# Twenty tail-value products moved into the first segment, tail rows loaded earlier, second scores placed inside a value chunk

## The chip, the cores and the metric

The kernel runs on one core of one Trainium2 chip. The metric is the device time of one execution in microseconds (us). A core has five engines that run beside each other and wait for each other through semaphores: TensorE (PE in the profile; its weight loads are listed apart as PEld), VectorE (DVE), ScalarE (ACT), GpSimd (POOL) and SyncE (SP), whose queue issues most of the transfers (DMAs).

## The reference, cut to what matters

The input x has 2048 rows of 640. The first block is a memory-augmented transformer with 32 heads of 128. The rows are cut into 64 segments of 32; ahead of each segment stand 8 memory rows, so that each attention covers 40 rows:

```
for s in range(64):
    h = concat([mem, layernorm(x)[32*s : 32*s + 32]])      # 8 + 32 rows
    q, k, v = h @ Wq, h @ Wk, h @ Wv                       # 640 -> 32 heads x 128
    p = softmax(mask(q @ k.T * scale));  o = (p @ v) @ Wo
    mem = o[:8];  outs.append(o[8:])
h  = x + concat(outs)
h2 = h + (relu(layernorm(h) @ w1 + b1)**2) @ w2 + b2       # w1: 640 -> 1728
```

Segment s + 1 needs the memory rows that segment s has produced: the 64 segments are a chain. The feed-forward part at the end is not.

## The kernel before, in words

**Sixteen blocks of four segments.** `step(b, sp)` works on segment s = 4b + sp. It projects 32 rows at a time: the 8 memory rows and the first 24 rows of the segment (`HD`). The last 8 rows of each segment, the tail rows (`TL`), depend on no memory; the tail rows of a whole block, four times 8, are projected together, as *tail units*: one unit is one 128-row chunk c of the contraction with four products of 128x32 by 128x512, which run beside each other in the four 32-column groups of PE. Ten units make the q, k or v of a block's tail rows (two halves n of five chunks). Finished v halves go through a row tile to a DRAM buffer `vt_d` (`tail_out`, L363) and come back per block as `vt`. Ten more units per block apply Wo to the tail rows of a block that is done.

**One step.** q and k of both halves (`project`, L498), with `first_half` (L609) inside the last of them: `scores(0)` and `soft1(0)`. Scores `sm` are those of the 8 memory queries only (16 small products, L526); the others, `token_scores`, are weighed a step later, off the chain. Then the value projection of half 0 into `ps0`, with `token_scores(0)` in its middle, `soft2(0)`, `scores(1)`, `soft1(1)`, `soft3`, whose four copies of 32 rows spread the transposed weights into `pB` (L566: g = 0 on DVE, g = 1 on ACT, g = 2 and 3 on POOL), then the value projection of half 1 into `ps1` in two pieces around `token_scores(1)` (L648 to L652). `values(0)` (weights times v, 20 products on PE), `values_out(0)` (a cast to `oT` on ACT), `values(1)`, and the output rounds `wo_rounds` into `pw`, whose first 16 products read the oT of half 0. `wo_out` (L298) turns pw into the next memory rows: two copies on ACT, a sum on DVE and a transpose into `hT` (L412), which the q projection of the next step reads. The weighted values of the 32 rows of the step before (`token_values`, on PE) come between.

**The filler.** Tail units and tail-output units are put into the list `fill`, which `step` empties at fixed places with `run(fill, n)`: (ahead - 1)//2 of them ahead of `values(0)` (L680), the rest of `ahead` between `values(0)` and the output rounds (L685), and what is left after the output rounds (L727). `ahead` is half of the list, rounded up (L678). How many a step gets is set by `portion(s)` (L951): the total up to step s is round(8.05 s), so mostly 8, from `plan`, sorted by due time, with an earliest step for each entry (L942 to L947).

**An instruction count per step.** `lack` (L590) keeps the number of PE products per step at 1911/5 = 382.2 on average, by splitting up to 12 sets of projection products per projection into halves of 256 columns. A split set streams the same columns in twice as many instructions.

**The front.** `start` (L845) projects v, q and k of the first 32 rows together with the tail rows of blocks 0 to 3, and fills with tail-v units of blocks 4 to 9; the first step then has `ready` set, projects nothing and runs only its chain, with 5 units left over (`run(fill, 10)`, L665; `SEG0` at L796 holds zeros). SP issues in program order: rows 0 to 127 of x, three chunks of Wv, tail rows of x for blocks 4 to 7 (group 1), a chunk of Wv, group 2, the last chunk, Wq, Wk, Wo, then the writes to vt_d. ACT's queue issues tail rows of group 0 and the memory rows `mem0` (L139, L140). DVE works in order: statistics of the first rows (`ln_stats(0)`, L905), spreading mem0 into o0 (L907), the normalisation `ln_norm(0)` (L193), the transpose of the memory rows (L412), and only then statistics and normalisation of tail group 0 (L914). PE transposes the rows (L210), ACT and DVE copy them out. Group 3 (tail rows of blocks 12 to 15) is loaded in the first blocks, by four small DMAs, and transposed by a DMA.

Of the kernel before, what the change touches and what calls it, by code (L numbers as in the profile page):

```python
# [16 lines left out]
def kernel(  # L17
# [107 lines left out]
    def load_tail_rows(g, eng=nc.sync):  # L125

        xt = s2.tile([128, D], BF16, tag="xt", name="xt")
        if g > 2:
            for b in range(4):
                eng.dma_start(out=xt[32 * b:32 * b + 32, :],  # L130
                              in_=x2d.rearrange("(b s t) d -> b t s d", s=4, t=SEG)[4 * g + b, HD:SEG, :, :])
        else:
            eng.dma_start(out=xt[:], in_=x2d.rearrange("(s t) d -> s t d", t=SEG)[16 * g:16 * g + 16, HD:SEG, :])
        xts["t", g] = xt
# [4 lines left out]
    load_tail_rows(0, nc.scalar)  # L139
    nc.scalar.dma_start(out=mem0[HD:SEG, :], in_=A_mem0[0])  # L140
    load_w(wv, A_Wv, 0, 3)
# [55 lines left out]
    def ln_transpose(b):  # L197

        xn = xns.pop(b)
        if not isinstance(b, tuple) and b > 0:  # L200
            nc.sync.dma_start(out=rows_in(b), in_=xn[:], transpose=True)
            return
        if isinstance(b, tuple) and b[1] > 2:
            hTt = s2.tile([128, DC, 4, TL, 4], BF16, tag="hTt", name="hTt", bufs=4)
            nc.sync.dma_start(out=hTt[:].rearrange("p c b k s -> p c (b k s)"), in_=xn[:], transpose=True)
# [23 lines left out]

    def proj(w, by, lhs, n, ps, c0, c1):  # L230

# [6 lines left out]
        for c in range(c0, c1):  # L238
            for k in range(4):
                out_, rhs, start, stop = ps[32 * k:32 * k + 32, :], wr[:, c, n, k], c == 0, c == DC - 1  # L240
                if owed[0] == 0 or start or stop:
                    matmul(out_, lhsT=lhs(c), rhs=rhs, start=start, stop=stop)
# [243 lines left out]
    def step(b, sp, v=None):  # L486
# [39 lines left out]
        def scores(n):  # L526
            sm = chn.tile([128, 512], F32, tag="ch", name="sm")
            for j, g in [(j, g) for a in range(2) for j in range(4) for g in (a, a + 2)]:
                p = n * 16 + g * 4 + j
                matmul(sm[32 * g:32 * g + 32, 0:NK], lhsT=qz[:, p, :], rhs=of(kT, p),  # L530
                       start=(j == 0), stop=(j == 3), skip_group_check=True)
            sms[n] = sm
# [28 lines left out]
        def soft3(pm):  # L561
            pT = s1.tile([128, 2, 32], BF16, tag="pTt", name="pT")[:].rearrange("p u k -> p (u k)")
            nc.vector.transpose(out=pT, in_=pm)
            def part(g):
                r = slice(32 * g, 32 * g + 32)
                (nc.vector.tensor_copy, nc.scalar.copy, nc.gpsimd.tensor_copy, nc.gpsimd.tensor_copy)[g](out=pBs[0][r, g], in_=pT[r])  # L566
            for g in range(1, G):
# [40 lines left out]

        def first_half():  # L609
            if not last:  # L610
                scores(0)
# [17 lines left out]
        def token_scores(n):  # L629
            skv = view()  # L630
            for j in range(4):
                for g in range(G):
                    matmul(skv[32 * g:32 * g + 32, n * 4 + j, :], lhsT=of(qT, n * 16 + g * 4 + j),
                                     rhs=of(kT, n * 16 + g * 4 + j), start=True, stop=True,
                                     skip_group_check=True)

        token_scores(0)
# [12 lines left out]
        token_scores(1)  # L650
# [13 lines left out]
        if ready:  # L664
            run(fill, 10)  # L665
            run_late(0, 100)
# [178 lines left out]
    def start():  # L845
# [43 lines left out]

        owed[0] = 72  # L890
        stream("q", wq, qT, lambda: ln_transpose(("t", 2))())
# [51 lines left out]
    for b in range(10, NB):  # L943
        u = tail_units(b, "v")
        plan += [(b - 8 if b < 12 else 28 + 4 * (2 * b - 24 + n), 1 if b < 12 else 7, u[DC * n:DC * n + DC]) for n in range(2)]
    for b in range(NB - 1):
# [4 lines left out]
    def portion(s):  # L951
        n = {NS - 3: 482, NS - 2: 486}.get(s, round(8.05 * s)) - paced[0]
        got = []
        while True:
# [6 lines left out]
            d, _, u = begun[0]  # L961
            if len(got) >= min(n, 9) and d > s:
                break
# [6 lines left out]
    for b in range(NB):  # L970
        for sp in range(4):
# [17 lines left out]
            if 0 < b < NB - 1 and sp == 1:  # L989
                ln_transpose(b + 1)  # L990
            if (b, sp) == (0, 3):
                load_tail_rows(3)
            if (b, sp) == (1, 0):
                late.insert(0, (1.15, lambda: ln_stats(("t", 3)), 4))
            if (b, sp) == (1, 1):
                mid.append(lambda: ln_norm(("t", 3)))
            if (b, sp) == (1, 2):
                ln_transpose(("t", 3))
            e = b * 4 + sp - (NS - 7)
# [144 lines left out]
```

## Time and profile before

| | us |
|---|---|
| median of three runs | 938.44 (937.07 to 940.75) |
| the profiled execution | 941.83 |
| its span in the trace | 940.0 |
| PE busy | 917.0 (98%) |
| PEld busy | 593.6 (63%) |
| DVE busy | 627.6 (67%) |
| ACT busy | 607.9 (65%) |
| POOL busy | 308.5 (33%) |

The profiled execution took 1.8 us more than its span. Busy time says which engine works, not whether it works at its rate: PE counts as busy while a product is under way, and products of neighbouring column groups overlap. The timeline lists start and duration of merged groups of instructions; an entry in brackets is the idle time of the engine before the group and what ended it. "SPq" rows are issues of transfers, not transfers.

### The profile page before, as it was taken

How to read it: one execution, taken by the hardware profiler on the slowest of the kernel's cores; microseconds unless marked ns; L12 is line 12 of the kernel's file. 1: busy time of each engine (PE TensorE's matmuls, PEld its weight loads, DVE VectorE, ACT ScalarE, POOL GpSimd, SP SyncE). 2: the span in 40 equal slices, each digit the busy share in tenths (PEclk: the TensorE clock that was granted, in tenths of full speed). 3: DMA queues.
4: the chain of work that ended last, by engine and by line, in shares of the span. 5: the costliest groups of instructions: out<-in, count | busy, mean ns of one | idle time of the engine just before them, and what ended most of it. 6: DMA issues, size and time to landing. Idle time of an engine off the chain costs nothing.

```text
span 940.0 us, 58306 instructions
## 1 busy us (share of the span) xinstructions
PE 917.0 (98%) x25889; PEld 593.6 (63%) x25900; DVE 627.6 (67%) x2068; ACT 607.9 (65%) x1586; POOL 308.5 (33%) x1003
## 2 busy tenths in 40 slices
PE   5989999999999999999999999999999999999998
PEld 2546666666666666666666666666666666565555
DVE  4257777767777677777777777767677777556632
ACT  1557777777777777777777777777777766524321
POOL 2123333333333333333333333333333343344300
PEclk9999999999999999999999999999999999999999
DMA  9982212020201010110102010101010221724320
GB/s 348 411 277 68 45 15 32 12 29 16 27 16 25 20 22 20 20 22 23 23 15 32 10 32 13 32 14 33 14 33 13 52 44 23 259 58 92 92 57 29
DMA packets 65820, 56.80 MB, mean 60 GB/s; under 512 B 37320, under 2 KB 61648, under 8 KB 63648
## 3 DMA queue, kind: packets, MB, share of 16 engines
q1 hardware_dynamic: 65280, 52.57, 21.1%
q8 instruction: 203, 3.33, 1.5%
q14 instruction: 49, 0.40, 0.2%
q10 hardware_dynamic: 160, 0.17, 0.1%
q0 software_dynamic: 128, 0.33, 0.1%
HBM read 38.37 MB, written 9.44 MB: 51 GB/s over the span
## 4 chain that ended last, share of the span: by engine, by line
PE 96%; DVE 2%; ACT 1%; DMA 1%; issue 1%; POOL 0%; ACTq 0%; DVEq 0%
PE ps L228 31%; PE px L228 22%; PE pw L228 16%; PE pk L228 7%; PE ps L1045 6%; PE po L228 5%; PE y L1101 4%; PE ps L1101 2%; PE sm L228 2%; PE pa L228 1%; DMA mem<-in_A_mem_dram 1%; DVE wk L1054 0%; ACT row L268 0%; DVE lnst L158 0%; PE pe L228 0%
## 5 line engine op out<-in xcount | busy, mean ns | idle before, releaser
L228 PEld LDWEIGHTS <-hT 128*32 128x32 bf16 x8764 | 218.8, 96 | 121.1 <-DVE hT L412 20.3
L228 PE MATMUL px<-wv,hT 128*32 128x512 bf16 x2520 | 173.4, 378 | 0.0
L228 PE MATMUL pw<-wo,oT 128*32 128x320 bf16 x4224 | 169.6, 299 | 0.3 <-ACT oT L259 0.2
L228 PEld LDWEIGHTS <-oT 128*32 128x32 bf16 x4224 | 112.5, 96 | 36.9 <-ACT oT L259 20.7
L711 POOL TENSOR_TENSOR pkt<-ek,rk 128x64 bf16<-128x64 bf16 x64 | 18.9, 295 | 254.6 <-ACT otmp L311 253.0
L282 DVE STREAM_TRANSPOSE qT<-row 128x256 f32<-128x256 f32 x128 | 56.8, 443 | 64.8 <-ACT row L266 64.7
L282 DVE STREAM_TRANSPOSE kT<-row 128x128 f32<-128x128 f32 (+1 forms) x191 | 68.0, 357 | 30.0 <-ACT row L268 19.0
L228 PE MATMUL ps<-wq,hT 128*32 128x512 bf16 x1266 | 81.2, 382 | 2.1 <-DVE hT L412 1.7
L228 PEld LDWEIGHTS <-hTt 128*32 128x32 bf16 x1976 | 59.7, 97 | 33.4 <-issue 6.1
L228 PEld LDWEIGHTS <-v 32*128 32x128 bf16 (+1 forms) x4064 | 58.5, 93 | 35.0 <-issue 24.7
L1053 ACT ACTIVATE wv<-ps,b1f 128x512 bf16<-128x512 f32 (+1 forms) x56 | 37.6, 671 | 65.9 <-PE ps L1045 65.1
L228 PE MATMUL ps<-wk,hT 128*32 128x512 bf16 (+1 forms) x1695 | 80.2, 327 | 0.0
L228 PE MATMUL px<-wq,hT 128*32 128x512 bf16 (+1 forms) x1895 | 79.3, 308 | 0.0
L228 PE MATMUL pk<-wk,hT 128*32 128x512 bf16 (+1 forms) x1252 | 77.6, 377 | 0.0
L463 ACT CAST oT<-po 128x512 bf16<-128x512 f32 x128 | 68.7, 589 | 12.1 <-PE po L228 5.8
L266 ACT ACTIVATE row<-ps 128x512 bf16<-128x512 f32 x93 | 69.2, 771 | 4.5 <-PE ps L228 3.3
L259 ACT CAST oT<-po 128x128 bf16<-128x128 f32 x126 | 33.4, 265 | 52.9 <-PE po L228 51.4
L475 POOL COPY qz<-qT 128x96 bf16<-128x96 bf16 x126 | 33.4, 265 | 103.8 <-DVE qT L282 102.7
L519 ACT CAST row<-ps 128x256 bf16<-128x256 f32 x126 | 48.4, 457 | 20.4 <-PE ps L228 20.4
L266 ACT ACTIVATE row<-px 128x512 bf16<-128x512 f32 x63 | 47.5, 754 | 21.3 <-PE px L228 21.3
L310 ACT COPY otmp<-pw 64x96 f32<-64x96 f32 (+2 forms) x129 | 28.8, 223 | 50.0 <-PE pw L228 29.6
L228 PEld LDWEIGHTS <-qz 128*32 128x32 bf16 x2016 | 40.0, 94 | 26.8 <-issue 12.1
(143 smaller groups left out, 1856.6 us busy)
## 6 DMA issues: line engine op xcount, KB each, us to landing
wv<-in_A_Wv_dram SPq DMA_DIRECT2D x5, 1024.0 KB
wq<-in_A_Wq_dram SPq DMA_DIRECT2D x5, 1024.0 KB
wk<-in_A_Wk_dram SPq DMA_DIRECT2D x5, 1024.0 KB
o_all<-o SPq DMA_DIRECT2D x256, 7.5 KB
wo<-in_A_Wo_dram SPq DMA_DIRECT2D x6, 640.0 KB
vt<-vt_d SPq DMA_DIRECT2D x15, 256.0 KB
xt<-in_A_x_dram SPq DMA_DIRECT2D x18, 160.0 KB
wq<-in_B_w_dram SPq DMA_DIRECT2D x1, 2080.0 KB
```

The costliest lines, as they stand in the source:

```text
L228: nc.tensor.matmul(*args, **kw)
L259: nc.scalar.copy(out=out_, in_=in_)
L266: nc.scalar.mul(out=paired(row), in_=ps.rearrange("p (s f) -> p s f", s=2), mul=scale)
L282: nc.vector.transpose(out=to[:, n * 8 + u0 * 4:n * 8 + u1 * 4, 0:32], in_=row.bitcast(F32).rearrange("p (h e) -> p h e", e=32)[:, u0 * 4:u ...
L310: nc.scalar.copy(out=five(tmp[0:64])[:, cs], in_=blocks(64, 128, 0)[:, cs])
L463: nc.scalar.copy(out=oTg[:, gs, :, :, 0:SEG], in_=po[1][h][:, :, 0:256].rearrange("p g (n j q) -> p g n j q", n=2, q=32))
L475: nc.gpsimd.tensor_copy(out=d[:, :, :, 0:120].rearrange("p s g (j f) -> p s g j f", j=3)[:, :, :, :, 0:M], in_=src[:, :, :, 0:3])
L519: nc.scalar.copy(out=paired(row[:])[:, :, fs], in_=ps[:].rearrange("p (s f) -> p s f", s=2)[:, :, fs])
L711: nc.gpsimd.tensor_tensor(out=pkt[:], in0=ek[:, :, SEG:NK], in1=rk[:].unsqueeze(2).to_broadcast([128, HG, TL]), op=ALU.mult)
L1045: nc.tensor.matmul(ps[:], lhsT=w1[:, c, fc * 128:(fc + 1) * 128], rhs=hnT[:, c, :], start=(c == 0), stop=(c == DC - 1))
L1053: nc.scalar.activation(out=r[:, 0:w], in_=ps[:, 0:w], func=ACT.Relu, bias=b1f[:, fc:fc + 1], scale=1.0)
L1101: nc.tensor.matmul(y[hh][:, 0:DH], lhsT=f1T[:, fc, k * 128:(k + 1) * 128], rhs=w2[:, fc, cs], start=(fc == 0 and q == 0), stop=(fc == FFUL ...
```

## The change

- The memory rows are issued by SP, second in its queue and ahead of Wv, rather than by ACT. The statistics of tail group 0 stand ahead of the spreading of mem0 on DVE.
- Tail group 3 is loaded by one DMA behind the first chunk of Wk, its statistics and normalisation stand between the q and the k part of `start`, and PE transposes it in the k part. Its four DMAs, its work and its DMA transpose in blocks 0 and 1 go.
- The tail-v units of blocks 10 and 11 may begin at step 0. `portion` gives step 0 twenty units and then 7.717 per step rather than 8.05. In step 0, 5 units are run at the old place, 16 between the output rounds and 4 after them.
- Of the filler of a later step, 4 units are always left for after the output rounds, the rest goes ahead of them.
- The first chunk of `ps1` is cut by columns into two parts (heads 0 and 3, heads 1 and 2); `scores(1)` stands between the parts. Scores go through all four column groups in turn for each j, rather than through two groups first and then the other two.
- The copy g = 3 of `soft3` goes from POOL to DVE.
- `lack` gets a constant of 43; 76 rather than 72 sets are split in the q part of `start`.

```diff
-        if g > 2:
-            for b in range(4):
-                eng.dma_start(out=xt[32 * b:32 * b + 32, :], in_=...)
-        else:
-            eng.dma_start(out=xt[:], in_=x2d...[16 * g:16 * g + 16, HD:SEG, :])
+        eng.dma_start(out=xt[:], in_=x2d...[16 * g:16 * g + 16, HD:SEG, :])
...
-    nc.scalar.dma_start(out=mem0[HD:SEG, :], in_=A_mem0[0])
+    nc.sync.dma_start(out=mem0[HD:SEG, :], in_=A_mem0[0])
...
-        if isinstance(b, tuple) and b[1] > 2:
-            hTt = s2.tile([128, DC, 4, TL, 4], BF16, tag="hTt", name="hTt", bufs=4)
-            nc.sync.dma_start(out=hTt[:]..., in_=xn[:], transpose=True)
-            hTts[b[1]] = hTt
-            return
...
-    def proj(w, by, lhs, n, ps, c0, c1):
+    def proj(w, by, lhs, n, ps, c0, c1, part=None):
...
+                if part is not None:
+                    js = slice(1, 3) if part else slice(0, 4, 3)
+                    matmul(out_.rearrange("p (j e) -> p j e", j=4)[:, js], lhsT=lhs(c), rhs=rhs[:, js],
+                           start=(start and part == 0), stop=False, skip_group_check=True)
+                    continue
...
-            for j, g in [(j, g) for a in range(2) for j in range(4) for g in (a, a + 2)]:
+            for j in range(4):
+                for g in range(G):
...
-   (nc.vector.tensor_copy, nc.scalar.copy, nc.gpsimd.tensor_copy, nc.gpsimd.tensor_copy)[g](...)
+   (nc.vector.tensor_copy, nc.scalar.copy, nc.gpsimd.tensor_copy, nc.vector.tensor_copy)[g](...)
...
-            lack = paces[0] + (1911 * (len(paces) - 1)) // 5 - issued[0]
+            lack = paces[0] + (1911 * (len(paces) - 1)) // 5 - issued[0] + 43
...
             pm0 = soft2(0)
+        if not ready:
+            ps1 = potile(1)
+            proj(wv, "half", lhs, 1, ps1, 0, 1, 0)
+        if not last:
             scores(1)
...
-            ps1 = potile(1)
-            proj(wv, "half", lhs, 1, ps1, 0, 2)
+            proj(wv, "half", lhs, 1, ps1, 0, 1, 1)
+            proj(wv, "half", lhs, 1, ps1, 1, 2)
...
-            run(fill, 10)
+            run(fill, SEG0[9])
...
-            ahead = 0 if ready else (len(fill) + 1) // 2
+            ahead = 0 if ready else max(len(fill) - 4, 0)
...
-    SEG0 = (0, 0, 0, 0, 0, 0, 0)
+    SEG0 = (0, 0, 6, 2, 2, 3, 3, 0, 0, 5)
...
-        owed[0] = 72
+        owed[0] = 76
...
+        ln_stats(("t", 3))
+        ln_norm(("t", 3))
...
-        stream("k", wk, kT)
+        stream("k", wk, kT, lambda: ln_transpose(("t", 3))())
...
     ln_stats(0)
+    ln_stats(("t", 0))
...
     mem_to_hT(o0, 0, 0)
-    ln_stats(("t", 0))
...
-    load_w(wk, A_Wk)
+    load_w(wk, A_Wk, 0, 1)
+    load_tail_rows(3)
+    load_w(wk, A_Wk, 1, DC)
...
-        plan += [(b - 8 if b < 12 else ..., 1 if b < 12 else 7, ...) for n in range(2)]
+        plan += [(0 if b < 12 else ..., b // 12, ...) for n in range(2)]
...
-        n = {...}.get(s, round(8.05 * s)) - paced[0]
+        n = {...}.get(s, round(20 + 7.717 * s)) - paced[0]
...
-            if len(got) >= min(n, 9) and d > s:
+            if len(got) >= min(n, 9 if s else 20) and d > s:
```

The inner places of `SEG0` stand ahead of the groups of output rounds of step 0, its last place is the old `run(fill, 10)`. The removed lines of the main loop (`load_tail_rows(3)` at block 0, its statistics, normalisation and DMA transpose in block 1) are not repeated here.

More of the change, by code (lines that the diff above doesn't have):

```diff
@@ L127, in load_tail_rows @@
         xt = s2.tile([128, D], BF16, tag="xt", name="xt")
-        if g > 2:
-            for b in range(4):
-                eng.dma_start(out=xt[32 * b:32 * b + 32, :],
-                              in_=x2d.rearrange("(b s t) d -> b t s d", s=4, t=SEG)[4 * g + b, HD:SEG, :, :])
-        else:
-            eng.dma_start(out=xt[:], in_=x2d.rearrange("(s t) d -> s t d", t=SEG)[16 * g:16 * g + 16, HD:SEG, :])
+        eng.dma_start(out=xt[:], in_=x2d.rearrange("(s t) d -> s t d", t=SEG)[16 * g:16 * g + 16, HD:SEG, :])
         xts["t", g] = xt
@@ L202, in ln_transpose @@
             return
-        if isinstance(b, tuple) and b[1] > 2:
-            hTt = s2.tile([128, DC, 4, TL, 4], BF16, tag="hTt", name="hTt", bufs=4)
-            nc.sync.dma_start(out=hTt[:].rearrange("p c b k s -> p c (b k s)"), in_=xn[:], transpose=True)
-            hTts[b[1]] = hTt
-            return
         pt = mm.tile([128, 1024], BF16, tag="mm", name="pt")
@@ L240, in proj @@
                 out_, rhs, start, stop = ps[32 * k:32 * k + 32, :], wr[:, c, n, k], c == 0, c == DC - 1
+                if part is not None:
[3 more added lines that the diff above has]
+                    continue
                 if owed[0] == 0 or start or stop:
-                    matmul(out_, lhsT=lhs(c), rhs=rhs, start=start, stop=stop)
+                    matmul(out_, lhsT=lhs(c), rhs=rhs, start=start, stop=stop, skip_group_check=(by == "half"))
                     continue
@@ L527, in scores @@
             sm = chn.tile([128, 512], F32, tag="ch", name="sm")
-            for j, g in [(j, g) for a in range(2) for j in range(4) for g in (a, a + 2)]:
-                p = n * 16 + g * 4 + j
-                matmul(sm[32 * g:32 * g + 32, 0:NK], lhsT=qz[:, p, :], rhs=of(kT, p),
-                       start=(j == 0), stop=(j == 3), skip_group_check=True)
+            for j in range(4):
+                for g in range(G):
+                    p = n * 16 + g * 4 + j
+                    matmul(sm[32 * g:32 * g + 32, 0:NK], lhsT=qz[:, p, :], rhs=of(kT, p),
+                                     start=(j == 0), stop=(j == 3), skip_group_check=True)
             sms[n] = sm
@@ L565, in part @@
                 r = slice(32 * g, 32 * g + 32)
-                (nc.vector.tensor_copy, nc.scalar.copy, nc.gpsimd.tensor_copy, nc.gpsimd.tensor_copy)[g](out=pBs[0][r, g], in_=pT[r])
+                (nc.vector.tensor_copy, nc.scalar.copy, nc.gpsimd.tensor_copy, nc.vector.tensor_copy)[g](out=pBs[0][r, g], in_=pT[r])
             for g in range(1, G):
@@ L609, in first_half @@
         def first_half():
+            if ready:
+                run(fill, SEG0[7])
             if not last:
@@ L635, in token_scores @@
                                      skip_group_check=True)
+        if ready:
+            run(fill, SEG0[8])
         token_scores(0)
@@ L944 @@
         u = tail_units(b, "v")
-        plan += [(b - 8 if b < 12 else 28 + 4 * (2 * b - 24 + n), 1 if b < 12 else 7, u[DC * n:DC * n + DC]) for n in range(2)]
+        plan += [(0 if b < 12 else 28 + 4 * (2 * b - 24 + n), b // 12, u[DC * n:DC * n + DC]) for n in range(2)]
     for b in range(NB - 1):
@@ L951, in portion @@
     def portion(s):
-        n = {NS - 3: 482, NS - 2: 486}.get(s, round(8.05 * s)) - paced[0]
+        n = {NS - 3: 482, NS - 2: 486}.get(s, round(20 + 7.717 * s)) - paced[0]
         got = []
@@ L990 @@
                 ln_transpose(b + 1)
[L991 to L998, printed above, removed]
             e = b * 4 + sp - (NS - 7)
```

## The prediction, made blind

> **What bounds the kernel now.** I read first the page (busy shares, the forty slices), then the timeline of the first 64 us, then that of one step in the middle, and last the same places of all steps.
>
> ```profile
> PE 917.0 (98%) x25889; PEld 593.6 (63%) x25900; DVE 627.6 (67%) x2068; ACT 607.9 (65%) x1586; POOL 308.5 (33%) x1003
> ...
> PE   5989999999999999999999999999999999999998
> DMA  9982212020201010110102010101010221724320
> ...
> q8 instruction: 203, 3.33, 1.5%
> ```
>
> PE is busy everywhere but in the first slices, where the transfers are too: the weights. So the time is PE's work plus PE's waits, and a moved product gains only where it fills a wait. The front shows two such places:
>
> ```profile
> 8.88 0.45 DVE L193 TENSOR_SCALAR xn<-xt,lnmv,lnrs 128x640 bf16<-128x640 bf16 x1
> ...
> 11.77 0.45 DVE L193 TENSOR_SCALAR xn<-xt,lnmv,lnrs 128x640 bf16<-128x640 bf16 x1 [1.00 <-POOL lnrs L166]
> ...
> 12.92 1.04 PE L228 MATMUL pa<-wv,hT 128*32 128x512 bf16 x8
> ```
>
> PE's first projection waits for the second normalisation (tail group 0), 2.9 us behind the first. Then step 0:
>
> ```profile
> 58.83 0.28 PE L228 MATMUL po<-pB,v 128*32 128x32 bf16 x16 [0.78 <-DVE pB L558]
> 58.93 0.24 PE L228 MATMUL po<-pB,vt 128*32 128x128 bf16 x4
> 59.06 2.56 PE L228 MATMUL pw<-wo,oT 128*32 128x320 bf16 x64
> 62.81 1.30 PE L228 MATMUL ps<-wq,hT 128*32 128x512 bf16 x20 [1.19 <-DVE hT L412]
> ```
>
> The output rounds run without a hole; the 1.19 us behind them wait for the new memory rows. A step in the middle:
>
> ```profile
> 483.04 0.83 PE L228 MATMUL px<-wv,hT 128*32 128x512 bf16 x12
> 483.12 0.62 DVE L282 STREAM_TRANSPOSE kT<-row 128x128 f32<-128x128 f32 x2
> 483.69 0.31 PE L228 MATMUL sm<-kT,qz 128*32 128x40 bf16 x11
> 483.82 0.40 PE L228 MATMUL px<-wv,hT 128*32 128x512 bf16 x2
> 484.66 0.51 POOL L566 COPY pB<-pT 32x64 bf16<-32x64 bf16 x2 [1.04 <-DVE pT L563]
> 485.22 0.27 PE L228 MATMUL po<-pB,v 128*32 128x32 bf16 x11
> 485.67 0.27 ACT L259 CAST oT<-po 128x128 bf16<-128x128 f32 x1
> 486.03 0.79 PE L228 MATMUL pw<-wo,oT 128*32 128x320 bf16 x16
> ```
>
> The second scores start as the two kT transposes end. From values(0) (485.22) to the output rounds are 0.80 us, in which three filler units run; the rounds need the cast, which starts 0.45 us after values(0). From one first k product (pk) to the next, 42 of the first 59 steps take 11.75 to 11.93 us, the others up to 12.15.
>
> **Part 1, the front: -3.2 us at PE's first projection.** mem0 makes DVE wait: it lands on DVE at 7.17, and four copies of 0.94 and four of 0.70 us stand ahead of xn at 8.88. Ahead of Wv on SP it lands behind x's first rows, whose statistics start at 2.98. DVE then has: statistics 2.98 to 4.11; those of group 0, whose last packets land at 4.26, from about 4.6 to 5.7 (0.88 + 0.21); the copies to 7.35; xn at 7.4, 1.5 earlier; 0.66 us of small work (0.18, 0.34, 0.14); xn of group 0 at 8.3 rather than 11.77, its POOL work done long before. That is -3.5. The price is on SP: the mem0 transfer waits for the clearing of mem0 on DVE, which ends at 1.18, and Wv, issued at 1.19, goes behind it, by about 0.45 us, and all weights with it. The last Wv chunk landed at 18.38 and was first used at 22.59; it lands at 18.9 and with some 0.4 us to the semaphore meets a use at 19.1. I take -3.2. By their packets, Wq and Wk had 5.9 to 7.4 us between landing and use; 3.2, 0.45, and 0.5 for group 3 (160 KB at the 0.4 MB/us of these slices) fit in.
>
> The profile's rows give a clock of 1.00 from 12 to 21 us, but sets of four 512-column products start 0.43 us apart until 18.28 and 0.216 after it. If the slow pace ended at 18.28 whenever PE begins, only half of the 3.2 would be kept. [...]
>
> **Part 2, step 0: +3.9 us of which 4.26 come back.** Five more transposes on PE in start cost 0.27 (five take 0.28 of PEld at 26.06); their evacuation, 1.03 us on ACT and 0.74 on DVE, lies in a stretch where ACT is half busy (11.0 of 22 us). The statistics of group 3 (1.6 us of DVE) fall where DVE has 3 of 22 us busy. Sixteen units of 0.213 (four products of 512 columns beside each other) between the output rounds are 3.41 us and fill nothing that is a hole now; the last four lie in the hole of 1.19 and are free. They hold up one thing: the evacuation of the third tail row on ACT (0.58) stands ahead of wo_out's copies, +0.25. Do they cover Wo? Its last packets land at 59.3 now, about 60.7 to 61 with 0.45 + 0.5 ahead of them and the semaphore; PE, 2.9 earlier at 56.1, reaches the last group at 61.9. So they do, with 1 us to spare; without them it would wait to 61. The first k product of step 1, at 63.93 now, comes at 63.93 - 3.2 + 0.27 + 3.41 + 0.25 = 64.7, **+0.75**. Four writes of rows to vt_d on SP are ahead of step 1's vt load and of two loads of x; the row ring of four lets the k row of step 1 wait for the fourth write (issued near 64.3, a few us for such writes); bounds 0 and 2 us, I take 0, as 128 KB writes of this shape at 62.5 were through by 65.5.
>
> **Part 3, the filler: -2.4 rather than -4.26 us.** The listing of PE's order gives 20 units (4.26 us) less after step 0; in 16 steps only two units (0.40 to 0.43 us) are left between values(0) and the rounds. Values(0) itself takes 0.163. With three units this is 0.80: no wait. With 0.533 us of units (values(0) at 414.25, rounds at 415.02) it is 0.765, 0.069 more than their work; with 0.400 (769.98 to 770.68) 0.705. So the cast's floor is 0.705 to 0.765, and two units would need 0.59. Each of these steps wins 0.04 to 0.10, not 0.213. I take 0.765, the row with the same 0.445 from values(0) to the cast as the tail units show. Where the rounds start late, values(1) and the rest take 0.043 less (values(1) to the last product 1.68 for 1.735, 0.01 back ahead of it). Behind the rounds the floor is the chain to hT: last round to first q is 1.486 us for units of 0.267 to 0.853, so four units are just enough; the change keeps 0.77 to 0.93 there. Summed step by step with these floors: -1.8, and -0.6 for values(1). Both ends: -4.3 (no floor) and -1.2 (none of the help of part 5).
>
> **Part 4, second scores: -2.7 us.** From the first product of scores(1) to that of token_scores(1) takes 0.577 (median), from scores(0) to token_scores(0) 0.534 for the same products; 0.043 in each of 60 steps, and in a dozen the scores come another 0.035 or so late: 3.2 in all. It is the second kT transpose: the old order could begin on the first one. With half a chunk ahead (four 256-column products, 0.109) PE comes at 483.79, the transposes have ended at 483.74; the new order needs both from its second product on. The split costs 0.003 a step by rows (six such sets take 0.655, three whole ones 0.648). Bounds: 0 (the wait stays) to -3.2. The strided halves are not in the trace; their columns are the same.
>
> **Part 5, the copy g = 3.** Scores end 0.012 later, and PE reaches values(0) 0.043 earlier, where POOL's second copy now ends 0.05 ahead of it (485.17, 485.22). On DVE the copy adds some 0.09 behind 484.56; ACT's at 485.06 is then last, and values(0) does not wait. Without it 0.05 a step, 2.9 us, would go. It is in part 3's floors (0.345 from the last value product to values(0) becomes 0.285).
>
> **Sum.** +0.75 - 2.4 - 2.7 = -4.4 us. The profiled 941.83 (span 940.0 and 1.8 around it) becomes 937.4; it lies 3.4 above the median, so on the median 938.44 I say **934.0**.
>
> **Rivals.** *The filler is worth its full time:* 4.3 for 2.4, 931.8; against it, the 0.765 row. *The front gives half or nothing* (tail rows of x or Wv late, the slow pace lasting to 18.28): 1.6 to 3.2 lost, 936.5; for it, the last Wv chunk with no slack. *The value chain gives part 4 back:* +2.9, 937; for it, slack of some 0.06. *Slower: pauses of PE's instruction stream.* Queue q8 brings 203 blocks of 16.4 KB for 52,033 instructions, one per 256. In 14 of 62 steps PE, by the start times of its products, pauses 0.14 to 0.47 us (mean 0.27) near row 194 of a block: in ten behind the last round (row 184 to 193 in most steps), in four shortly ahead of it. After the change the last round has row 190 to 230, mostly above 196, so the pause falls within the rounds, ahead of the chain to hT. Should it come in every step there, 48 more times 0.27 make +13, 947; it turns slower from 17 more such pauses. Against: of the 19 old steps with a row above 194, four paused in the rounds, no larger a share than ten of the others. [...] *The change doesn't do what it says:* the listing has the scores between the halves, and 20 units in step 0.
>
> **How the numbers follow.** Forecast 0.48 (own range 932 to 936), full filler 0.15, front 0.20, value chain 0.08, pauses 0.09. About 0.5% (4.7 us) can be told from no change. Half of the forecast and the full filler are beyond it: 0.39; slower 0.09; the rest 0.52. The range 930.5 to 938.5 leaves out the pauses and the tails.
>
> **What would show it.** First projection at 9.5 to 9.9; first pk near 64.7; scores(1) to token_scores(1) 0.534; values(0) to the rounds 0.77 in the two-unit steps; as many pauses as now. Wrong would be: pk of step 1 past 66, or a rounds' end with pauses in most steps.

## The result

| | before | after |
|---|---|---|
| median of ten runs | 938.74 us (937.07 to 940.75) | 943.07 us (940.67 to 949.17) |
| the profiled execution | 941.83, span 940.0 | 943.79, span 941.7 |
| start of the first projection | 12.92 | 9.40 |
| start of the first k product (pk) of step 1 | 63.93 | 66.38 |
| from there to the end of the 61 steps behind it | 724.2 | 723.8 |

The ratio is 1.0050 (95% interval 1.0035 to 1.0065): slower, by 4.3 us, where 934.0 had been forecast. The profiled execution of before lies 3.1 us above its median, that of after 0.7, so the two profiles differ by less than the medians do. The first projection did start earlier, yet step 1 started later, and the chain behind it took as long as before. The next two parts follow the front and the chain.

### The front and step 0

The timeline of the first 22 us after the change (start, duration, engine, line, operation; in brackets the idle time ahead and what ended it):

```profile
7.38 0.33 DVE L407 STREAM_TRANSPOSE hT<-o 128x160 bf16<-128x160 bf16 x1
...
9.40 1.04 PE L218 MATMUL pa<-wv,hT 128*32 128x512 bf16 x8
...
12.56 0.38 PE L218 MATMUL pv<-wv,hTt 128*32 128x512 bf16 x4
...
17.12 0.61 PE L218 MATMUL pa<-wv,hT 128*32 128x512 bf16 x8 [0.73 <-DMA wv<-in_A_Wv_dram]
...
20.10 0.62 PE L218 MATMUL pa<-wv,hT 128*32 128x512 bf16 x8 [1.07 <-DMA wv<-in_A_Wv_dram]
```

PE starts 3.5 us earlier and then waits twice for Wv. By the packets of the trace the last two chunks of Wv were through at 15.36 and 18.33; PE got them at 17.12 and 20.10, 1.76 us later each time. In the trace the end of each of these loads is 16 increments of a semaphore. For the fourth chunk 15 of them had come by 16.04, the last at 17.08; for the last chunk 14 had come by 18.95, the other two at 20.03 and 20.06: PE waited for the last ones. In the thirteen profiles of kernels with the new front, the waits for Wv ended 1.4 to 3.0 us after the last packet. Step 0, from the timeline of PE:

```profile
57.24 1.50 PE L218 MATMUL pw<-wo,oT 128*32 128x320 bf16 x32
58.57 1.47 PE L218 MATMUL ps<-wv,hTt 128*32 128x512 bf16 x24
...
63.64 1.03 PE L218 MATMUL ps<-wv,hTt 128*32 128x512 bf16 x15
65.25 1.30 PE L218 MATMUL ps<-wq,hT 128*32 128x512 bf16 x27 [0.58 <-DVE hT L407]
66.38 1.26 PE L218 MATMUL pk<-wk,hT 128*32 128x512 bf16 x32
```

The rounds begin 1.82 us earlier than before (59.06), not 2.9, and from there to the first q product (the group with the bracket) takes 8.01 us instead of 3.75: 4.26 more. That is as much as twenty units take, though only sixteen stand there; the rest is explained further down.

### The chain

Two steps of after side by side, PE in the timeline. First one that runs without a break in its output rounds (pw), then the step before it, 12 us earlier:

```profile
181.91 0.23 PE L218 MATMUL po<-pB,vt 128*32 128x128 bf16 x4
181.97 1.82 PE L218 MATMUL pw<-wo,oT 128*32 128x320 bf16 x48
183.62 1.12 PE L218 MATMUL ps<-wo,oTt 128*32 128x320 bf16 x28
```

```profile
169.47 0.23 PE L218 MATMUL po<-pB,vt 128*32 128x128 bf16 x4
169.53 1.81 PE L218 MATMUL pw<-wo,oT 128*32 128x320 bf16 x45
171.85 0.32 PE L218 MATMUL pw<-wo,oT 128*32 128x320 bf16 x3 [0.51 <-issue]
171.87 1.17 PE L218 MATMUL ps<-wk,hTt 128*32 128x512 bf16 x16
```

The same in the weight loads (PEld), which go ahead of the products:

```profile
170.08 0.93 PEld L218 LDWEIGHTS <-oT 128*32 128x32 bf16 x30 [0.17 <-ACT oT L254]
171.86 0.10 PEld L218 LDWEIGHTS <-oT 128*32 128x32 bf16 x2 [0.85 <-issue]
```

After 30 of the last weight loads PE stands still for 0.85 us with "issue" as the releaser: it waits for nothing that the profile shows. The profile's page says the same of all steps in one line; first before, then after (busy us, mean ns, then idle time ahead and its releaser):

```profile
L228 PE MATMUL pw<-wo,oT 128*32 128x320 bf16 x4224 | 169.6, 299 | 0.3 <-ACT oT L259 0.2
```

```profile
L218 PE MATMUL pw<-wo,oT 128*32 128x320 bf16 x4224 | 174.2, 300 | 5.5 <-issue 3.8
```

Setting the steps side by side by the start times of their products shows the pauses. The stretch from the first values(1) product to the last round takes 1.682 us where nothing disturbs it (before 1.735), that from the last round to q 1.487; what a step takes beyond that is counted as pause. Of 60 steps, before has 14 pauses, of 3.7 us in sum, ten of them behind the rounds; **after has 24, of 11.1 us, all but 0.1 us of it in the rounds** (counted from the first values(1) product), the longest 1.0 us. The steps without a pause became shorter, as forecast: their median was 11.78 us and is 11.67.

That these are late instruction blocks can be read from the transfers. Queue q8, which the page lists as "instruction", made 204 transfers of 16.4 KB in this profile. PE has 52,301 records in it (26,036 weight loads, as many products, 229 of its sequencer), 256.4 for each transfer, so a block is counted here as 256 instructions of PE; the *row* is an instruction's place in its block. Among the 22 gaps of over 0.33 us between weight loads of one group that wait for no semaphore, all 22 stand at row 194 or 195 of a block, and PE goes on 1.24 to 1.56 us after the end of a q8 transfer. In no run of this case did PE pass that row of a block sooner than 1.1 us after the end of the transfer ahead of it. Three steps of after (those that begin at 150.41, 197.93 and 162.08 us), times in us from their first k product, from the packets of q8 and the weight loads:

```
begin    q8 transfers                          row 194 in the rounds: reached, left
150.41   1.59-2.77   5.84-6.95   9.52-10.59    no pause
197.93   1.79-2.74   6.80-7.79  10.79-11.67    8.78, 9.22
162.08   1.53-2.76   6.92-8.38  10.89-12.00    8.83, 9.78
```

The transfer ahead of the rounds starts at 5.8 in the step without a pause and at 6.8 or later in the other two, and its end decides. In 59 steps of this profile row 194 falls in the rounds: in 36 of them that transfer has ended by 7.37 us, and none pauses by over 0.1 us; in the other 23 it ends at 7.79 or later, and all pause. In the chain the next transfer never starts sooner than 2.18 us after the end of the one before, and all but one in twenty take 0.88 to 1.4 us (the longest 1.9). From start to start a round of this supply takes at least 3.2 us in all runs, with a median of 3.8, and a step of 11.7 us needs three rounds.

### The profile page after: what moved, and what is told of

Same layout as the page of the kernel before. It is cut to its first block, busy times and chain, and to the rows that moved or that the text cites. A ratio compares the mean times of both kernels' runs of the same rounds, so it can differ in the third digit from the quotient of the medians.

```text
span 941.7 us, 58591 instructions
## 1 busy us (share of the span) xinstructions
PE 917.9 (97%) x26036; PEld 559.9 (59%) x26036; DVE 635.9 (68%) x2132; ACT 612.5 (65%) x1587; POOL 294.8 (31%) x940
## 4 chain that ended last, share of the span: by engine, by line
PE 95%; DMA 1%; DVE 1%; ACT 1%; issue 1%; SPq 0%; ACTq 0%
PE ps L218 30%; PE px L218 22%; PE pw L218 16%; PE pk L218 7%; PE ps L1045 6%; PE po L218 5%; PE y L1101 4%; PE ps L1101 2%; PE sm L218 1%; DMA wv<-in_A_Wv_dram 1%; PE pa L218 1%; DVE lnst L153 0%; DMA xt<-in_A_x_dram 0%; PE pe L218 0%; ACT row L263 0%
## 5 line engine op out<-in xcount | busy, mean ns | idle before, releaser
L218 PEld LDWEIGHTS <-hT 128*32 128x32 bf16 x8891 | 209.2, 96 | 135.4 <-DVE hT L407 22.0
L218 PE MATMUL pw<-wo,oT 128*32 128x320 bf16 x4224 | 174.2, 300 | 5.5 <-issue 3.8
L218 PE MATMUL px<-wv,hT 128*32 128x512 bf16 x2772 | 167.5, 358 | 0.0
L218 PEld LDWEIGHTS <-oT 128*32 128x32 bf16 x4224 | 104.0, 96 | 56.7 <-ACT oT L254 25.5
L218 PE MATMUL px<-wq,hT 128*32 128x256 bf16 (+1 forms) x1874 | 79.3, 309 | 0.0
L218 PEld LDWEIGHTS <-v 32*128 32x128 bf16 (+1 forms) x4064 | 48.1, 93 | 43.4 <-issue 24.9
L307 DVE TENSOR_TENSOR o<-pw,otmp 128x96 bf16<-128x96 f32 (+2 forms) x129 | 31.3, 243 | 43.5 <-ACT otmp L306 37.5
```

Of the source, the lines that this page charges most:

```text
L218: nc.tensor.matmul(*args, **kw)
L307: nc.vector.tensor_tensor(out=five(o[:])[:, cs], in0=blocks(0, 128, 32)[:, cs], in1=five(tmp[:])[:, cs], op=ALU.add)
```

## The experiments

The ratios are to the kernel before, measured in the same batch, with 95% intervals; medians in us of different batches should not be compared. Pauses are counted as above, in one profiled execution each; how they vary between executions of one kernel is not shown.

### Where the block boundary falls

The constant of `lack` decides how many sets are split in the first few steps: 43 more with the change than with C = 0, 37 fewer with -37. Everything behind them is shifted within the blocks, and neither what is computed nor its order changes:

```diff
-            lack = paces[0] + (1911 * (len(paces) - 1)) // 5 - issued[0] + 43
+            lack = paces[0] + (1911 * (len(paces) - 1)) // 5 - issued[0] + C
```

C = 32:

> The changed kernel with the constant of lack 32 instead of 43: 11 products (22 rows of PE's instruction stream) fewer, so that in the 59 middle steps row 194 of a 256-row instruction block falls inside the output rounds in 10 steps instead of 55, and behind the last round in the others. Theory (the 23 pauses of mean 0.47 us inside the rounds are fetches of the next instruction block, and they hurt because of where row 194 falls): pauses in the rounds drop from 23 to at most 6, the time to 936 to 938 us. Rival (the block comes late because the new order and the transfers delay the fetch, wherever row 194 falls): as many pauses, now behind the rounds, 941 to 944 us.

C = 0:

> The changed kernel with the constant of lack 0, as in the kernel before: 86 rows fewer, row 194 falls between the first values product and the first output round in 56 of 59 steps, and in the rounds in 3. Theory (place of row 194): the sixteen small score products and the twenty of values(0) pass before it, so the 256 rows behind it are used up fast; pauses appear between values(0) and the rounds, in some of the steps only, 936 to 941 us. Rival (place does not matter): 941 to 944 us with some 23 pauses.

C = 107:

> The changed kernel with the constant of lack 107: 128 rows more than now, row 194 falls in the first third of the output rounds in all 59 steps. Theory (place of row 194): pauses inside the rounds in at least 20 steps again, earlier in the rounds, 941 to 945 us. Rival (place does not matter): 941 to 944 us. This run does not part the two by its time, but by where the pauses are and how long: by the theory they vary with the number of rows between the projections and the place, by the rival they keep 0.47 us.

C = -15:

> The changed kernel with the constant -15: 30 rows from constant 0, row 194 stands among the first products of the output rounds in 53 steps instead of ahead of them. Theory (a late block costs nothing where PE waits for the cast anyway, 0.17 us between values(0) and the rounds, and costs its full length behind it): more pauses in the rounds than with constant 0 (7), 15 or more, 940 to 943 us. Rival (the distances in time between the crossings decide, and they are nearly the same): 937 to 939.5 us.

C = -37:

> The changed kernel with the constant -37: row 194 stands some 60 rows into the output rounds in 58 steps, and the next crossing close ahead of the first q product of the next step, where PE waits 0.39 us for the memory rows. Theory (place): pauses in the rounds, none behind them, 939 to 943 us. Rival (distances in time): 937 to 939.5 us.

| C | median, us | ratio (interval) | pauses in the profile, us: from values(1) to the last round, behind, elsewhere |
|---|---|---|---|
| 107 | 944.12 | 1.0042 (1.0023 to 1.0061) | 1.7, 3.9, 1.0 |
| 43 (the change) | 943.07 | 1.0050 (1.0035 to 1.0065) | 11.0, 0, 0.1 |
| 32 | 940.76 | 1.0014 (1.0003 to 1.0026) | 2.4, 3.0, 0 |
| 0 | 938.09 | 0.9983 (0.9971 to 0.9995) | 1.3, 0.4, 2.3 |
| -15 | 947.52 | 1.0065 (1.0047 to 1.0083) | 0.1, 11.0, 0.1 |
| -37 | 963.44 | 1.0249 (1.0223 to 1.0274) | 22.4, 2.2, 0.3 |

The same work in the same order, and 25 us between the best and the worst place, by the ratios. The worst run, -37, even has the fewest instructions of the six, so the split sets themselves are not what costs. With -37 the pauses stand among the products of values(1):

```profile
182.99 0.23 PE L218 MATMUL po<-pB,v 128*32 128x32 bf16 x10
183.54 0.22 PE L218 MATMUL po<-pB,v 128*32 128x32 bf16 x6 [0.32 <-issue]
183.59 0.24 PE L218 MATMUL po<-pB,vt 128*32 128x128 bf16 x4
```

and on the page of its profile values has the idle time that the rounds had:

```profile
L218 PE MATMUL po<-pB,vt 128*32 128x128 bf16 x504 | 31.1, 218 | 7.5 <-issue 7.5
```

So the place decides; the rival that it does not is out. How much a place costs I could not foresee: of the five expectations only that for C = 0 came true in time and in the place of the pauses. C = 32 was expected at 936 to 938 us and took 940.76, since its pauses moved behind the rounds; C = -37 was expected at 939 to 943 and took 963.44. C = 107 lies in its range, but its profile has 1.7 us of pauses in the rounds, not pauses in 20 steps, and lost 4 to 5 us in the front (it waited 2.65 us for Wv): a mixed case. What I expected of C = -15 was half wrong: the time rose, but the 31 pauses came at the next crossing of row 194, behind the rounds. Neither "hidden where PE waits anyway" nor the distances in time between the three crossings of a step orders the runs (medians by the weight loads: 3.1, 3.9 and 4.7 us with C = 0; 3.4, 3.8 and 4.5 with the change; 3.3, 3.6 and 4.9 with -15; 3.8, 3.9 and 4.5 with -37). What the place does to a transfer's start stays open.

A second test of the supply: fewer rows, and more.

```diff
-                extra[one] = min(max(lack, 0), 12)
+                extra[one] = 0        # no split sets; for the other run: 12
```

No splits:

> The changed kernel without the sets split for the pace (lack gives none; the 76 of the start stay): 740 rows of PE per step instead of 768, so 2.89 blocks instead of 3, and row 194 drifts through all places of a step, in the rounds in 40 cases, between values(0) and the rounds in 13, behind the rounds in 64. Theory (fetch of blocks): the pauses stand at row 194 wherever it is in a step, are rare where projections stand ahead of it, and each is shorter as the fetches are 4% rarer: pauses in the rounds in 10 to 18 steps, 936 to 941 us. Rival (pauses come from the steps with large transfers, each fourth): they stay in the same steps as now, 941 to 944 us.

All split:

> The changed kernel with 12 sets split in each of the four q and k projections of every step: 836 rows of PE per step instead of 768, 3.27 instruction blocks instead of 3, the same columns streamed. Theory (PE is held by the transfer of blocks: the next transfer starts at the earliest 2.3 us after the end of the one before, a transfer takes 0.88 to 1.4 us, and no PE instruction of the new block runs sooner than 1.2 us after its end): three and a quarter such rounds of 3.3 to 3.9 us fill the step of 11.7 us, so that pauses come in most steps, 950 to 970 us. Rival (the pauses are not from the supply of blocks): 943 to 946 us, the added products costing what split sets cost by the rows of before.

Without splits 942.74, 1.0033 (1.0021 to 1.0045), 10.6 us of pauses in 27 steps, in the rounds in 19 steps, behind them in 7, where 936 to 941 us and 10 to 18 steps were expected: 3.6% fewer instructions in the chain do not help when the boundary drifts through all places. The rival of that run was that the pauses come from the steps with large transfers, each fourth. In the changed kernel they do come more often there: 11 of 23, and the steps with a pause have 446 KB of other transfers on average, those without 153. Without splits every fourth step has 6 of 25 pauses (250 KB with a pause, 273 without), so large transfers are not needed for a pause; whether they make a block later stays open. With all sets split 975.48, 1.0376 (1.0350 to 1.0402): 31 us over the change by the ratios, for instructions that stream the same columns, with 30.7 us of pauses in 51 steps of its profile; the theory had said 950 to 970. That PE is held by the supply of instructions is shown by this run together with those of the constant.

The kernel before at the best place:

```diff
-            lack = paces[0] + (1911 * (len(paces) - 1)) // 5 - issued[0]
+            lack = paces[0] + (1911 * (len(paces) - 1)) // 5 - issued[0] - 36
```

> The kernel before with the constant of lack -36 (last round at median row 119 instead of 191, row 194 between values(0) and the rounds in 58 steps), nothing else: the kernel before at the place where the changed kernel was best. Theory (fetches of instruction blocks hurt less there, as PE waits for the cast of values(0) at that place anyway): its own pauses shrink by 1 to 3 us, 936 to 938 us. Rival (the place helps only the new order): 939 to 941 us.

938.46, 0.9996 (0.9986 to 1.0006). Its pauses fell to 0.9 us in two steps, but the time did not fall measurably, against the 936 to 938 us of the theory: at its own place the kernel before loses little.

### The parts one by one

**The front**, alone on the kernel before:

```diff
-    nc.scalar.dma_start(out=mem0[HD:SEG, :], in_=A_mem0[0])
+    nc.sync.dma_start(out=mem0[HD:SEG, :], in_=A_mem0[0])
...
     ln_stats(0)
+    ln_stats(("t", 0))
...
     mem_to_hT(o0, 0, 0)
-    ln_stats(("t", 0))
```

> The kernel before with the front alone: memory rows issued by SP ahead of Wv, statistics of tail group 0 ahead of the copies of mem0. PE's instruction stream is unchanged, so pauses should be as before. Theory (in the changed kernel the front is 3.5 us early at the first projection, but the last two chunks of Wv take 1.75 us from their last packet to PE, and with no filler in step 0 the output rounds then wait for Wo, whose last packets land at 59.3 in both): first projection near 9.4, end of the Wv part 2.5 us earlier, first k product of step 1 at 63.0 to 63.9 instead of 63.93, time within 1 us of the kernel before. Rival (the front is worth what it gains at the Wv part, nothing behind it is late): 61.4 to 62 for that product and 2 to 2.5 us less in all.

940.60, 1.0016 (1.0006 to 1.0027), first pk at 64.38: nothing gained, rather 1.5 us lost. The rounds of its step 0 did not wait for Wo, as the theory had said they would. Its timeline shows what the theory had left out:

```profile
19.18 0.38 PE L228 MATMUL pv<-wv,hTt 128*32 128x512 bf16 x4
21.59 0.72 PE L228 MATMUL pa<-wv,hT 128*32 128x512 bf16 x8 [2.03 <-DMA wv<-in_A_Wv_dram]
22.06 1.11 PE L228 MATMUL pa<-wv,hTt 128*32 128x512 bf16 x8
22.91 1.53 PE L228 MATMUL ps<-wv,hTt 128*32 128x512 bf16 x12
```

Behind the wait of 2.03 us PE is at half pace again: eight products take 0.85 us (22.06 to 22.91) instead of 0.43, until about 25.4. In this profile the early start only moves the wait to Wv, and behind that wait the full pace is gone for some 3 us; how many of the other executions lost the pace is not on record. And in the changed kernel with C = 0, the same lines back as they were:

> The changed kernel with constant 0 (938.1 us) and the old front: memory rows issued by ACT, statistics of tail group 0 behind the transpose of the memory rows. Theory (the last chunks of Wv, 1.75 us from their last packet to PE, take back most of the early start): first projection near 12.9, first k product of step 1 0.5 to 1.5 us later than 66.9, time 938.5 to 940 us. Rival (the front keeps the 3.2 us of the prediction): 941 us.

938.94, 0.9993 (0.9982 to 1.0005), against 0.9983: the front is worth some 0.9 us there by the ratios, not 3.2, and the intervals overlap. In this pair of profiles the first pk comes 1.8 us later with the old front (68.69 for 66.90).

**The filler**, undone in the changed kernel:

```diff
-    SEG0 = (0, 0, 6, 2, 2, 3, 3, 0, 0, 5)
+    SEG0 = (0, 0, 0, 0, 0, 0, 0, 0, 0, 10)
...
-            ahead = 0 if ready else max(len(fill) - 4, 0)
+            ahead = 0 if ready else (len(fill) + 1) // 2
...
-        n = {...}.get(s, round(20 + 7.717 * s)) - paced[0]
+        n = {...}.get(s, round(8.05 * s)) - paced[0]
```

(and the plan's earliest steps of blocks 10 to 15 as before.)

> The changed kernel with the old filler (blocks 10 and 11 from step 1, 8.05 units a step, half of them ahead, no units between the rounds of step 0) and the constant -49, so that the last round has the median row 119 as with constant 0 (118). Theory (20 units cost 3.4 us in step 0, of which about 1.5 cover a wait for Wo anyway, and give back 3 to 4 us in the chain): 938.5 to 940 us, with the first k product of step 1 near 64.5 to 65.5 instead of 66.9. Rival (the filler was worth its full 4.26 us and cost little): 941 to 942 us; other rival (it gave nothing): 936 us.

937.43, 0.9971 (0.9958 to 0.9984), against 0.9983 and below the 938.5 to 940 us expected: nothing is lost without it, the intervals overlap. In the profiles step 0 ends 1.2 us earlier (pk at 65.70 for 66.90; the rounds then wait for Wo twice, 0.54 and 0.47 us), and the 61 steps behind take 2.2 us more.

**The second scores and the copy**, alone on the kernel before, at its own place in the blocks (C = -4) and at the best one (C = -40), with the new order of scores and the copy on DVE:

```diff
+            proj(wv, "half", lhs, 1, ps1, 0, 1, 0)
             scores(1)
...
-            proj(wv, "half", lhs, 1, ps1, 0, 2)
+            proj(wv, "half", lhs, 1, ps1, 0, 1, 1)
+            proj(wv, "half", lhs, 1, ps1, 1, 2)
```

> The kernel before with parts 4 and 5 alone: the scores(1) inside the first chunk of ps1, their order over all four column groups, the copy g = 3 on DVE; the constant of lack is -4, so that the last round keeps the place in the instruction blocks that it has before (median row 191; row 194 in the rounds in 24 steps, before 22). Theory (the score part gains 0.045 us a step, the 0.055 that values(0) then waits longer comes back as the shorter rounds): step 2.5 to 3 us shorter in sum, 935.5 to 937 us. Rival (value chain takes it back): within 0.5 us of the kernel before.

> The kernel before with parts 4 and 5 alone (as in f2, 941.0 us there) and the constant -40, which puts the last round at median row 119 and row 194 between values(0) and the rounds in 58 steps. Theory (at this place the blocks cost little, and the score part keeps its 0.045 us a step): 2.5 to 4 us below the kernel before at the same place (ratio 0.9996), so 935 to 937 us. Rival (the shorter step is given back to the blocks here too): 938 to 941 us.

Own place: 941.00, 1.0029 (1.0017 to 1.0041), slower where 935.5 to 937 us had been expected, with 7.3 us of pauses for 3.7, though its steps without a pause are shorter (median 11.71 us for 11.78). Best place: **936.48, 0.9955 (0.9940 to 0.9969)**, by the ratios 3.9 us below the kernel before at that place. It beats both kernels and is the lowest of all versions, though the interval overlaps with those of the next run and of the old filler above. With the front added:

> The same with the front (memory rows on SP, statistics of group 0 early). Theory (front alone was worth nothing: 64.38 against 63.93 at the first k product, as waits for Wv set PE's pace back and Wo is late at step 0): within 1 us of h1. Rival (the 1.0 us that the front was worth with constant 0): 1 to 2 us below h1.

937.52, 0.9964 (0.9951 to 0.9976): no further gain. In the changed kernel, old scores and old copy (the reverse of that edit), C = 4:

> The changed kernel with the old second scores and the copy g = 3 on POOL again (parts 4 and 5 undone) and the constant 4, which keeps the rows of the rounds as with constant 0 (median row 118). Theory (at this place of the blocks the score part is worth its 0.045 to 0.09 us a step): 940.5 to 943 us. Rival (whatever a step gets shorter by is given back to the supply of blocks): 937.5 to 939 us, with undisturbed steps 0.05 to 0.1 us longer and fewer pauses.

940.54, 1.0014 (0.9999 to 1.0028) against 0.9983: 2.9 us for the scores and the copy together. Last the copy g = 3 alone, back on POOL, with C = 0:

```diff
-   (nc.vector.tensor_copy, nc.scalar.copy, nc.gpsimd.tensor_copy, nc.vector.tensor_copy)[g](...)
+   (nc.vector.tensor_copy, nc.scalar.copy, nc.gpsimd.tensor_copy, nc.gpsimd.tensor_copy)[g](...)
```

> The changed kernel with the constant 0 and the copy g = 3 back on POOL; PE's instructions are those of the run with constant 0 (938.1 us). Theory (the copies on POOL end last, as the prediction worked out for part 5): values(0) waits another 0.03 to 0.06 us a step behind the last value product, 0 to 3 us more, 938 to 941 us. Rival (the copy on DVE is what made values(0) wait 0.058 us longer than before): that wait falls from 0.199 to 0.14 us behind the filler unit, and the time to 935 to 937 us.

939.59, 1.0009 (1.0000 to 1.0018) against 0.9983: the wait ahead of values(0), behind its filler unit, grows from 0.199 to 0.271 us, in 60 steps 4.3 us, of which 2.4 arrive in the time. So the new scores with the old copy (1.0009) cannot be told from the old scores with the old copy (1.0014): the scores show a gain only together with the copy.

## Why the prediction was wrong

**The pauses: the step that failed.** The rival "pauses of PE's instruction stream" had the mechanism, the queue, the row and nearly the place, and got a chance of 0.09. What failed is the step that left this term at nothing, "as many pauses as now", on the count against it ("of the 19 old steps with a row above 194, four paused in the rounds, no larger a share than ten of the others"): 24 steps pause after the change, and by 0.46 us on average, not 0.27. Why the old steps were no sample of the new ones is not shown; all three crossings in a step moved together, so more changed than the row in the rounds. By C = 43 against C = 0, with no other edit, this term is 0.67% or 6.3 us. The rival's own price of 13 us came near the 11.1 us of pauses by luck: it had twice as many pauses, about half as long. In the changed kernel most of the three crossings of each step show no pause, but 24 in 60 steps do and cost 11 us, and with C = -37 it is over 20, so the measurement decides against leaving them out of a sum.

**Part 1, the front: the mechanism right, the size wrong.** The first projection came at 9.40 (forecast 9.5 to 9.9). The price on Wv did not show (last packet at 18.33, before 18.38). The mis-sized term is the 0.4 us "to the semaphore": it was 1.76. At the last chunk 2.5 us were left of 3.5 (22.59 to 20.10), at the start of the rounds 1.8: the five transposes (0.27), 0.2 us ahead of them and 0.3 us in the Wq part lie between, and 0.1 us comes back behind them. The half pace (sets of four products 0.40 to 0.43 us apart) ended at 12.56 instead of 18.28, behind it they are 0.215 apart; so in this run the doubt whether it would stay until 18.28 was for nothing. The 3.2 us was kept whole on the assumption that it would end earlier with an earlier start, which the profile of before does not show. Over all runs it ended between 15.4 and 18.4 with the old front and between 12.3 and 15.4 with the new: both spread over some 3 us, and the later start has the later ends. What ends it is not shown.

**Part 2, step 0.** Forecast +3.9 with +0.75 left at the first pk; it came at 66.38 instead of 64.7. Of these 1.7 us, 1.1 are the front and 0.6 the units: they took 4.26 from the rounds to q rather than 3.66, because a pause of 0.3 us at row 194 and later ACT copies put the last round back. Wo was in time, as forecast; without the units, in the run with the old filler, the rounds wait for it. A first pk past 66 stood on the prediction's own list of what would be wrong.

**Part 3, the filler: right in size, but not net.** Two-unit steps take 0.711 from values(0) to the rounds, less than the 0.765 chosen. The chain gained 2.2 us in the pair of profiles (forecast 2.4), one execution each, and step 0 paid 1.2 of it; in time nothing was measured. The rival at full price (4.3 for 2.4) should have read 932.1, not 931.8; nothing hangs on that.

**Part 4, second scores: right together with part 5.** From the first score of half 0 to values(0) a step takes 2.566 for 2.611, 0.045 less. From scores(1) to token_scores(1) it takes 0.428, and 0.537 with the half chunk of 0.109 that now stands ahead, where 0.534 had been forecast. The two pairs at the good place give 2.9 and 3.9 us, forecast 2.7, but both change the copy too. The prediction had said that without the copy 2.9 us would go; with the copy alone undone 2.4 go. At the place of the kernel before the gain was lost to pauses.

**Part 5, the copy: right in what the old one would cost, wrong that values(0) does not wait.** It waits 0.058 longer than before (0.199 for 0.141), and the rounds get 0.053 back, since values(1) then waits for nothing. The rival "the value chain gives part 4 back" so came about and cost nothing.

**The sum.** Against the forecast span of 935.6, the profile shows 941.7: 1.7 from the front and step 0, 7.4 more of pauses than in the profile of before, and, as the rest, 3.0 better elsewhere. Against the medians 3.0 more are missing, mostly because the profiled run of before lies further above its median than that of after; its number of pauses may be why, but only one run of it has a profile. The medians give a sum that does not lean on that profile. With C = 0 the pauses (4.0 us) are as many as before (3.7 us), and the time is 0.9983 of before: 1.6 us gained where 4.7 had been forecast from the median of 938.74. So of the 9.1 us between 934.0 and 943.07, 6.3 come with the place of the blocks and 1.7 with the front and step 0; 1.1 us, less than the width of the intervals, stays open.

## What to carry to other kernels

Where an engine works 98% of the time on many small instructions, as PE does here, look at its supply of instructions too: divide the instructions per step by those of a block (256 in these traces), compare with the measured round of the supply (here at least 3.2 us, and mostly 3.5 to 4.0 in the run with all sets split), and try several offsets before judging any edit that moves instructions, since the offset alone made 25 us here. Of a gain at the start of a stretch that waits for transfers, count no more than the slack of the last transfer in it (here 2.5 of 3.5 us were left), taken from its last packet plus the time until the engine sees it (here 1.4 to 3.0 us).

## What the runs showed of the hardware that was not expected

- PE never passed row 194 of a 256-instruction block sooner than 1.1 us after the end of the transfer ahead of it; the transfers (16.4 KB, all but one in twenty 0.88 to 1.4 us) started 2.2 us or more after the end of the one before. Splitting sets, which streams no more columns, cost 31 us for 68 rows more per step.
- After waits of 2.03 us (front alone) and 2.65 us (C = 107) for Wv PE fell back to half pace for some 3 us; after waits of up to 1.74 us in eleven other runs it did not.
- From the last packet of a 1 MB load to the first product that waited for it 1.76 us passed, twice in one run, and 1.4 to 3.0 us over the thirteen profiles of the new front. One or two late ones of the 16 semaphore increments made it so long where they were read: the last came at 20.06 after the change, for a product at 20.10, and at 21.55 in the run of the front alone, for a product at 21.59.
